# Column tiles for the small matmuls of a segment loop, a whole output projection, and a shorter last segment

## The chip, the cores and the metric

The kernel runs on one core of a Trainium2 chip. The metric is the device time in microseconds of one execution.

## The reference

Two branches read the same `x` (2048 tokens of 512): a recurrent attention `A` and a feed-forward `B`, mixed by a gate. Only `A` bears on this case. It goes through 64 segments of 32 tokens, and each segment needs the 8 memory rows that the previous one produced.

```python
mem = mem0                                    # 8 rows
for s in range(64):
    h = concat([mem, x[32*s : 32*s+32]])      # 40 rows
    q, k, v = h @ Wq, h @ Wk, h @ Wv          # 32 heads of 128
    p = softmax(mask(q @ k.T * scale))
    o = (p @ v) @ Wo                          # 4096 -> 512
    mem = o[:8]                               # needed by the next segment
    outs.append(o[8:])
return g * concat(outs) + (1 - g) * B(x)      # B: layernorm, two linear layers, gelu
```

## The kernel before

Each pass of the loop handles one segment. What is needed for the next memory comes first, and other work (output projections of the tokens, projections of later tokens, the branch `B`) fills the gaps as "side work". TensorE writes its results into banks of a memory called PSUM, and VectorE, ScalarE or GpSimd copy or work on them; one engine tells another that it is done through a semaphore, a counter that the other waits for. Four segments make one tile of 128 tokens, and `si` is the segment's place in its tile. The parts that the change and the argument touch, in the order in which TensorE runs them:

```python
# first sums: softmax denominators of the memory rows (one 128x128 tile)
nc.tensor.matmul(sm[:], lhsT=BO[:], rhs=E[:, :, 8:16], start=True, stop=False)
nc.tensor.matmul(sm[:], lhsT=BO[:], rhs=E[:, :, 0:8], start=False, stop=True)
run_fill(5 + (si == 3))                                   # side work
nc.vector.reciprocal(out=R[:, 0:8 * NG]..., in_=sm[:])
nc.vector.tensor_tensor(out=Pm[...], in0=E[..., 0:16], in1=R[...], op=ALU.mult)
av(Um, 8, s, V, Pm, 8, 0, 0)                              # value product, 32x128 tiles
# second sums: denominators of the other rows, into the mask's bank (bank 7)
nc.tensor.matmul(sr, lhsT=BO[:], rhs=E[:, :, 16:48], ...)
nc.tensor.matmul(sr[:, :, 24:32], lhsT=BO[:], rhs=E[:, :, 48:56], ...)
...                                                       # UTT <- Um, four copies
nc.vector.reciprocal(out=R[:, 8 * NG:]..., in_=sr)        # 256 columns
for half in range(2):                                     # projection of the memory rows, two halves
    wp = bank((nb, nd)[half], [P, 256])
    for u in range(8):
        wo_unit(wp, UTT[Tp % 2], ..., 256 * half, 256 * half + 256)   # 128x32 tiles
    (nc.scalar.copy if half else nc.vector.tensor_copy)(out=wsb[:, d], in_=wp[:])
S_next = mask_mm()                                        # mask into bank 7, one 128x128 tile
av_x(s - 1, ...)                                          # value product of the other rows
run_fill(2 * (si == 3))
for m in range(KC):                                       # memory output, four 128x128 tiles
    nc.tensor.matmul(aT[:, m, :], lhsT=wsb[:, m * P:(m + 1) * P], rhs=Sel[:, 0:M], ...)
nc.vector.tensor_copy(out=hn[:, :, 0:M], in_=aT)          # hT: the next segment's memory
for _ in fill: pass                                       # rest of the side work
```

## Time and profile before

| | before |
|---|---|
| median time | 835.74 us (3 runs, 835.13 to 835.79) |
| span of the profiled execution | 832.9 us |
| TensorE busy | 804.7 us, 97% |
| mean iteration, mask to mask | 11.19 us |
| from the last segment's first projection to the end | 26.6 us |

The mean iteration leaves out the first four. The last row of the table is 832.9 minus 806.32, the start of the last segment's first projection. A 97% busy TensorE says only that a matmul is always in flight. What is lost shows in the distances between starts where the tile shape changes. The prediction below shows those lines.

### The profile page before, as it was taken

What the parts mean: (1) busy time and instruction counts of PE and PEld (TensorE: products, weight loads), DVE (VectorE), ACT (ScalarE), POOL (GpSimd) and SP (SyncE); (2) the same over time, 40 slices, a digit from 0 to 9 for tenths busy, and PEclk for the clock granted to TensorE, in tenths of its full rate; (3) what the DMA queues carried; (4) which work ended last, traced back from release to release, by engine and by line L of the source; (5) the groups of instructions that cost most, each with busy time, mean ns of one, the idle gap of its engine ahead of it and who ended that gap; (6) DMA issues with size and microseconds to landing.
All of it is one profiled execution on the core that took longest, in us unless ns stands there. A gap on an engine that the chain in (4) does not pass through costs nothing.

```text
span 832.9 us, 49239 instructions
## 1 busy us (share of the span) xinstructions
PE 804.7 (97%) x22405; PEld 495.4 (59%) x22417; DVE 501.7 (60%) x1019; ACT 434.0 (52%) x1245; POOL 273.7 (33%) x625
## 2 busy tenths in 40 slices
PE   6999999999999999999999999999999999999886
PEld 4665555665666665566566556656656656665554
DVE  5764256565666566666656565656656665666553
ACT  3555544555455555555554555455555555555552
POOL 8000234242424333332424242434243243424220
PEclk9999999999999999999999999999999999999999
DMA  9791210100000010101010100000010101010000
GB/s 318 253 391 44 87 32 7 28 12 24 15 23 23 17 28 10 37 11 35 10 27 13 35 11 22 23 20 26 12 34 10 36 10 35 5 35 5 10 5 24
DMA packets 38216, 37.64 MB, mean 45 GB/s; under 512 B 13545, under 2 KB 36434, under 8 KB 36466
## 3 DMA queue, kind: packets, MB, share of 16 engines
q1 hardware_dynamic: 37874, 34.31, 12.4%
q8 instruction: 177, 2.90, 1.5%
q14 instruction: 37, 0.30, 0.1%
q0 software_dynamic: 128, 0.13, 0.1%
HBM read 26.03 MB, written 6.29 MB: 39 GB/s over the span
## 4 chain that ended last, share of the span: by engine, by line
PE 93%; DVE 3%; DMA 1%; issue 1%; SPq 1%; ACT 1%; DVEq 0%; ACTq 0%
PE b L211 35%; PE b L233 18%; PE b L222 17%; PE b L384 5%; PE hp L456 4%; PE bp L473 4%; PE b L360 2%; PE b L369 2%; PE b L684 2%; PE b L719 1%; PE b L389 1%; PE b L673 1%; DMA Wo_sb<-in_A_x_dram 1%; PE b L320 1%; PE b L373 0%
## 5 line engine op out<-in xcount | busy, mean ns | idle before, releaser
L217 DVE STREAM_TRANSPOSE Tt<-b 128x512 f32<-128x512 f32 (+1 forms) x384 | 225.6, 613 | 85.5 <-PE b L211 71.8
L211 PEld LDWEIGHTS <-hT 128*32 128x32 bf16 x5120 | 134.7, 97 | 100.0 <-DVE hT L720 15.4
L233 PE MATMUL b<-Wo_sb,UTT 128*32 128x256 bf16 (+1 forms) x4736 | 162.7, 285 | 1.2 <-ACT UTT L619 0.8
L222 PE MATMUL b<-Wv_sb,hT 128*32 128x512 bf16 x2048 | 141.9, 379 | 0.0
L211 PE MATMUL b<-Wq_sb,hT 128*32 128x512 bf16 x2048 | 132.9, 380 | 1.4 <-DVE hT L720 1.4
L211 PE MATMUL b<-Wk_sb,hT 128*32 128x256 bf16 (+1 forms) x3072 | 133.3, 308 | 0.0
L233 PEld LDWEIGHTS <-UTT 128*32 128x32 bf16 x4736 | 121.4, 97 | 19.1 <-ACT UTT L619 1.5
L654 ACT CAST KT<-Tt 128x256 bf16<-128x256 f32 (+1 forms) x192 | 87.1, 476 | 53.6 <-DVE Tt L217 53.6
L605 POOL TENSOR_TENSOR Px<-E,R 128x256 bf16<-128x256 bf16 x64 | 43.0, 672 | 218.7 <-DVE R L689 218.7
L689 DVE RECIPROCAL R<-b 128x256 f32<-128x256 f32 x64 | 112.5, 1757 | 0.0
L654 POOL CAST QT<-Tt 128x512 bf16<-128x512 f32 x64 | 39.1, 611 | 192.6 <-DVE Tt L217 192.6
L619 ACT CAST UTT<-b 128x256 bf16<-128x256 f32 x256 | 76.8, 387 | 23.9 <-PE b L389 23.4
L708 ACT CAST wsb<-b 128x256 bf16<-128x256 f32 x66 | 24.6, 372 | 120.1 <-PE b L233 120.1
L677 DVE RECIPROCAL R<-b 128x64 f32<-128x64 f32 x64 | 35.6, 557 | 79.4 <-PE b L674 79.4
L654 ACT CAST QT<-Tt 128x512 bf16<-128x512 f32 x64 | 39.6, 619 | 66.7 <-DVE Tt L217 66.7
L384 PEld LDWEIGHTS <-V 32*128 32x128 bf16 x4096 | 35.3, 91 | 46.2 <-DVE Pm L679 32.0
L222 PEld LDWEIGHTS <-hT 128*32 128x32 bf16 x2048 | 49.5, 96 | 21.1
L688 ACT CAST UTT<-b 128x64 bf16<-128x64 f32 x128 | 20.9, 215 | 75.2 <-PE b L389 75.2
L461 ACT ACTIVATE hg<-hp,b_sb 128x256 bf16<-128x256 f32 x80 | 37.7, 473 | 38.9 <-PE hp L456 38.9
L456 PE MATMUL hp<-yT,w_sb 128*128 128x256 bf16 (+1 forms) x352 | 53.8, 278 | 2.8 <-ACT hg L461 1.5
L607 POOL TENSOR_TENSOR racc<-racc,R 128x320 f32<-128x320 f32 x64 | 55.5, 867 | 0.0
L720 DVE CAST hT<-b 128x32 bf16<-128x32 f32 x63 | 12.1, 191 | 62.4 <-PE b L719 61.6
(116 smaller groups left out, 1075.2 us busy)
## 6 DMA issues: line engine op xcount, KB each, us to landing
Wv_sb<-in_A_Wv_dram SPq DMA_DIRECT2D x4, 1024.0 KB
Wq_sb<-in_A_Wq_dram SPq DMA_DIRECT2D x4, 1024.0 KB
Wk_sb<-in_A_Wk_dram SPq DMA_DIRECT2D x4, 1024.0 KB
Wo_sb<-in_A_Wo_dram SPq DMA_DIRECT2D x2, 2048.0 KB
vd<-vt SPq DMA_DIRECT2D x32, 128.0 KB
vs<-vd SPq DMA_DIRECT2D x256, 16.0 KB
out_dram<-o SPq DMA_DIRECT2D x16, 128.0 KB
Wo_sb<-in_A_x_dram SPq DMA_DIRECT2D x1, 1024.0 KB
```

The costliest lines, as they stand in the source:

```text
L211: nc.tensor.matmul(bk[32 * j:32 * j + 32, 0:n], lhsT=G[:, kc, :], rhs=W5[t][:, kc, h0:h1, j, :], start=(kc == 0), stop=(kc == KC - 1), til ...
L217: nc.vector.transpose(out=Tt[:, 0:n], in_=bk[:, 0:n])
L222: nc.tensor.matmul(bk[32 * j:32 * j + 32, :], lhsT=G[:, kc, :], rhs=Wv5[:, kc, 4 * vb:4 * vb + 4, j, :], start=(kc == 0), stop=(kc == KC - ...
L233: nc.tensor.matmul(bk[32 * g:32 * g + 32, :], lhsT=ut[:, i, j, c0:c0 + 32], rhs=Wo_sb[:, 4 * i + j, d0:d1], start=(j == 0 and i < 4), stop ...
L384: nc.tensor.matmul(U[j][:, i, :], lhsT=V[q, i, :], rhs=Pt[q, i, c_main:c_main + n], start=(i == 0), stop=False, skip_group_check=True, til ...
L456: nc.tensor.matmul(hp[:rows, :], lhsT=w1_sb[:, kc, fc * P:fc * P + rows], rhs=yTs[blk][:, kc, :], start=(kc == 0), stop=(kc == KC - 1))
L461: nc.scalar.activation(out=hg_[:rows, :], in_=hp[:rows, :], func=ACTF.Gelu_apprx_tanh, bias=b1_sb[:rows, fc:fc + 1], scale=1.0)
L605: nc.gpsimd.tensor_tensor(out=Px[:, :, 0:32], in0=E[:, :, 16:48], in1=Rr, op=ALU.mult)
L607: nc.gpsimd.tensor_tensor(out=racc[:], in0=racc[:], in1=R[:], op=ALU.add)
L619: nc.scalar.copy(out=UTT[T % 2][:, :, j, c0 + M:c0 + 40], in_=U[:])
L654: (nc.gpsimd.tensor_copy if bi == 2 else nc.scalar.copy)(out=dst, in_=Tv)
L689: nc.vector.reciprocal(out=R[:, 8 * NG:].rearrange("p (i q) -> p i q", q=32), in_=sr)
```

## The change

TensorE loses 0.10 to 0.11 us where the tile shape changes (the prediction reads this off the lines), and the loop mixed three shapes: 128x32 for the projections, 32x128 for the value products, 128x128 for sums, mask and memory output. The change writes those last three as 128x32 tiles. It also makes the memory projection one pass of 512 columns instead of two of 256, cuts the product `Pm` in two so that its first half is ready sooner, and reworks the end: the last segment computes no memory (nobody reads it), its output projections run in line, and the last output leaves in two column halves.

```diff
+    def sums(o, rhs, start, stop):
+        for j in range(4):
+            q = slice(32 * j, 32 * j + 32)
+            nc.tensor.matmul(o[q], lhsT=BO[:, q], rhs=rhs, start=start, stop=stop, ..., tile_position=(0, 32 * j))
+    def mem_out(aT, wsb):
+        for m in range(KC):
+            for c in range(4):
+                nc.tensor.matmul(aT[32 * c:32 * c + 32, m, :], lhsT=wsb[:, m * P + 32 * c:m * P + 32 * c + 32], rhs=Sel[:, 0:M], ..., tile_position=(0, 32 * c))
     def mask_mm():
-        nc.tensor.matmul(S, lhsT=ident[:], rhs=MkA[:]..., start=True, stop=True)
+        for j in range(4):                                    # q as in sums
+            nc.tensor.matmul(S[q], lhsT=ident[:, q], rhs=MkA[:]..., tile_position=(0, 32 * j))
 ... in the loop
-            nc.tensor.matmul(sm[:], lhsT=BO[:], rhs=E[:, :, 8:16], start=True, stop=False)   # and three more
+        sums(sm, E[:, :, 8:16], True, False)                                                 # and three more
-            nc.vector.tensor_tensor(out=Pm[...], in0=E[:, :, 0:16]..., in1=R..., op=ALU.mult)
+        for c in (8, 0):
+            nc.vector.tensor_tensor(out=Pm[:, :, c:c + 8], in0=E[:, :, c:c + 8], in1=R[:, 0:8 * NG]..., op=ALU.mult)
-        for half in range(2): ... wo_unit(wp, ..., 256 * half, 256 * half + 256)
-            (nc.scalar.copy if half else nc.vector.tensor_copy)(out=wsb[:, d], in_=wp[:])
+        wp = bank(nb, [P, Dm])
+        for u in range(8):
+            wo_unit(wp, UTT[Tp % 2], 24 - 8 * sp, u)
+        nc.scalar.copy(out=wsb[:], in_=wp[:])
-            for m in range(KC): nc.tensor.matmul(aT[:, m, :], lhsT=wsb[:, m * P:(m + 1) * P], ...)
+            mem_out(aT, wsb)
 ... the PSUM banks are taken in another order, as the projection now needs one in place of two
 ... the last segment leaves the loop after its scores; some 60 lines of its own end follow
```

## The prediction

> **What bounds the kernel now.** I read the page first (busy shares, then the chain that ended last), then the timeline of TensorE, VectorE and ScalarE over one inner iteration, then the groups by shape for the durations.
>
> ```profile
> PE 804.7 (97%) x22405; PEld 495.4 (59%) x22417; DVE 501.7 (60%) x1019; ACT 434.0 (52%) x1245; POOL 273.7 (33%) x625
> PE 93%; DVE 3%; DMA 1%; issue 1%; SPq 1%; ACT 1%; DVEq 0%; ACTq 0%
> ```
>
> TensorE is busy for 97% of the span and is 93% of the chain. No other engine is near. So the question is how much of TensorE's time is streaming and how much is something a different tiling can remove. One iteration (one segment of 32 tokens, about 11.2 us; 64 of them) in TensorE's timeline; columns are start us, length us, instruction, count:
>
> ```profile
> 520.26 0.82 PE L222 MATMUL b<-Wv_sb,hT 128*32 128x512 bf16 x12
> 521.01 0.20 PE L673 MATMUL b<-E,BO 128*128 128x64 bf16 x1
> 521.05 0.19 PE L674 MATMUL b<-E,BO 128*128 128x64 bf16 x1
> 521.18 1.05 PE L211 MATMUL b<-Wq_sb,GL 128*32 128x512 bf16 x16
> 522.05 0.39 PE L211 MATMUL b<-Wk_sb,GL 128*32 128x512 bf16 x4
> 522.37 0.36 PE L384 MATMUL b<-Pm,V 32*128 32x8 bf16 x32
> 522.59 0.23 PE L389 MATMUL b<-Pm,VL 32*128 32x32 bf16 x8
> 522.75 0.28 PE L684 MATMUL b<-E,BO 128*128 128x256 bf16 x1
> 522.87 0.19 PE L685 MATMUL b<-E,BO 128*128 128x64 bf16 x1
> 522.99 0.40 PE L211 MATMUL b<-Wk_sb,GL 128*32 128x512 bf16 x4
> 523.22 1.92 PE L233 MATMUL b<-Wo_sb,UTT 128*32 128x256 bf16 x64
> 525.07 0.36 PE L360 MATMUL b<-MkA,ident 128*128 128x448 bf16 x1
> 525.37 0.37 PE L384 MATMUL b<-Px,V 32*128 32x32 bf16 x32
> 525.58 0.24 PE L389 MATMUL b<-Px,VL 32*128 32x32 bf16 x8
> 525.75 0.26 PE L719 MATMUL b<-Sel,wsb 128*128 128x8 bf16 x4
> 525.94 0.62 PE L211 MATMUL b<-Wk_sb,GL 128*32 128x512 bf16 x8
> ```
>
> To be seen: four column-tiled (128*32) matmuls run side by side, since 16 of 512 columns (521.18 to 522.05) take 0.87 us, 0.216 per wave of four. A wave of 256 columns takes 0.109: 16 waves of L233 are 1.75 us. Now compare starts where the tile shape changes. L222's three waves should end at 520.26 + 0.65 = 520.91, but L673 (128*128) starts at 521.01: 0.10 late. L233 should hand over at 524.97; the mask L360 starts at 525.07: 0.10 late. L360's 448 columns stream in 0.19, but L384 (32*128) follows after 0.30: 0.11 late. L685's 64 columns (0.03) take 0.12. Where the shape stays (L211 to L233) nothing is lost. So each change of tile shape costs about 0.1 us, and there are nine per iteration.
>
> **What the Trainium skill says.** "TensorEngine Tiling (Array Packing)", Tiling Modes, Key Properties: "Changing tiling mode (not just tile) drains the TensorE". The trace agrees and gives the size: 0.10 to 0.11 us. "TensorE: Matmul & The Clock Gate", Part 3, says tiles in different column groups run concurrently; it agrees (0.216 us for four of 512). "ScalarE: Activation LUTs", What ACT_TABLE_LOAD costs, gives 0.833 ns per element; the page's groups agree, 372 ns for a 256-column copy out of PSUM and 585 for 512, the difference being 256 x 0.83. "VectorE: DVE Perf Modes", TRN2 errata, gives (N+151)/0.96 ns for a two-input fp32 operation: 291 at N=128, trace 292; so I take 225 ns for N=64.
>
> The waits that can replace a removed switch are in these lines of VectorE and then ScalarE over the same stretch:
>
> ```profile
> 521.28 0.56 DVE L677 RECIPROCAL R<-b 128x64 f32<-128x64 f32 x1 [1.64 <-PE b L674]
> 521.95 0.29 DVE L679 TENSOR_TENSOR Pm<-E,R 128x128 bf16<-128x128 bf16 x1
> 522.88 0.36 DVE L688 CAST UTT<-b 128x64 bf16<-128x64 f32 x2 [0.65 <-PE b L389]
> 523.17 1.76 DVE L689 RECIPROCAL R<-b 128x256 f32<-128x256 f32 x1
> ```
>
> ```profile
> 520.73 0.19 ACT L670 ACTIVATION_READ_ACCUMULATOR E<-b 128x1 f32 x1
> 525.19 0.37 ACT L708 CAST wsb<-b 128x256 bf16<-128x256 f32 x1 [1.95 <-PE b L233]
> ```
>
> **The change part by part, per iteration.** The sums (L673, L674, L684, L685), the mask (L360) and the memory output (L719) become 128*32 tiles, four matmuls in place of one, same columns, so the streaming time is the same. Of nine switches five go: into and out of the first sums, out of the second sums, into the mask, out of the memory output. Four stay, around the two value products (L384/L389). Five times 0.1 is 0.5 us; times 63 iterations, 31 us. That is the ceiling. What is left of each, in the order of the timeline:
>
> (a) First sums. Entry: 0.106 goes, but E's accumulator read ends at 520.92 and a consumer follows a release by about 0.055 (the hT copy ends 526.24, its weight load starts 526.29), so the sums can start at 520.975 in place of 521.01: 0.035. Exit: 0.16 from L673 to the next L211 becomes 0.04 + 0.02: 0.10. Together 0.135. The next value product needs Pm. VectorE's reciprocal starts with the sums, 0.035 earlier, and the product is cut in two, only the first half (225 ns) needed at once: Pm at 522.14 + 0.055, TensorE free at 522.24. So 0.135 is kept, except in every fourth iteration, where GpSimd copies VL at the same time and the product takes 0.40 (its product of 128 columns is 403 ns there): about 0.05.
>
> (b) Second sums. 0.104 goes between L684 and L233. But L233 needs the UTT copy: VectorE's first one ends near 523.11 and L233's load starts 0.055 later, 523.16, for a matmul at 523.22. Only 0.055 is kept.
>
> (c) Whole projection. 8 waves of 512 in place of 16 of 256: same streaming. The start of the last wave comes 0.13 earlier (7 x 0.216 + 0.01 = 1.52 against 1.65). Before, half 0 left during half 1 and only 372 ns of ScalarE lay behind the end. Now all 512 columns do: from the last start 0.45 to ScalarE's start (a 512-column matmul record is 0.38, and L708 starts 0.07 after such an end), 0.585 copy, 0.06 to the weight load. So memory output at 1.52 + 0.45 + 0.585 + 0.06 = 2.62 after the first L233, against 525.75 - 523.22 = 2.53. The mask's saved switch vanishes into this wait and 0.09 is lost. In the iteration with si = 3 two units of fill (0.44 us) stand between and cover the copy; there the mask waits for VectorE's 1.76 us reciprocal, which frees its bank: it starts at 2.35 after the value product in place of 2.435, and with the fill's switch (0.106) gone too, (b) and (c) together give 0.20.
>
> (d) Memory output. 16 small matmuls at 6 ns take 0.09 as the four did; the 0.08 of the switch out of it is saved. The hT chain behind it (matmul 0.17, copy 0.19, waits) is 0.45, the two units of fill 0.46: it just fits. With si = 3 one unit of fill is left and hT binds as before: 0.
>
> Sum for four iterations (si = 0, 1, 2, 3): 0.18 + 0.18 + 0.10 + 0.33 = 0.79 us. 63 iterations: 12.4 us.
>
> (e) The end. Before, from the last segment's first projection (806.3) to TensorE's last load of the check flag (827.3) are 21.0 us, with several stretches of TensorE waiting on ScalarE and VectorE. Adding the new order up with the same durations (no memory part; three projections of 1.73, the last output in two halves of 0.87; ScalarE copies of 0.585 between them; the check's count done early) I get 19.2. So 1.7 us; the 5.6 us behind it stay.
>
> (f) Scattered stalls of 0.2 to 0.4 us on TensorE ("issue" before L384, some 3 us in all) stay; where they fall before the memory output the new wait hides them: perhaps 0.5 us.
>
> Total 12.4 + 1.7 + 0.5 = 14.6 us: 835.7 - 14.6 = 821.1.
>
> **Rivals.** First: the waits behind the switches are softer than I read them, and most of the 0.5 us is kept. For it: every saved switch also shifts the work that feeds the waits. Against it: E, UTT and wsb hang on ScalarE and VectorE, whose lines show 0.035, 0.055 and less than nothing of slack. It would give 805 to 812. Second: the exposed copy costs more than 0.09 (ScalarE at 0.63 as in its back-to-back copies, or hT missing its fill by a hair), in three of four iterations, and eats the rest: 826 to 833. For it: (d) fits by 0.01 us only. Third: VectorE becomes the bound through the mask's bank, in all iterations. Against it: the wait for wsb comes 0.1 later than that one. It would change nothing in the sum. Fourth: only the end gets faster (834).
>
> **Range and chances.** The sum is made of terms of 0.05 to 0.1 us repeated 63 times, so an error of 0.05 us per iteration is 3 us. I take 821 with 816 to 826. Faster by over 2% means under 819.0, which needs 2 us more than I find: 0.28. Within 2%: 0.70. Slower: 0.02.
>
> **What would show it.** In the after trace: L673's successors start 0.03 us earlier against ScalarE's read, followed by fill with no gap; the weight loads of the memory output wait for ScalarE's wsb copy in three iterations of four, 0.1 to 0.2 us each, with that copy at 0.585 us; L233's load waits for UTT; the mask waits for the reciprocal in si = 3; a mean iteration (mask to mask) of about 11.02 us in place of 11.22. I am wrong if the memory output does not wait for wsb (then 812 or less), or if the new tiles themselves take longer than the ones they replace.

## The result and the profile after

| | before | after |
|---|---|---|
| median time (same rounds, 4 runs each) | 835.51 us | 822.74 us (822.18 to 822.87) |
| span of the profiled execution | 832.9 us | 821.1 us |
| mean iteration, mask to mask | 11.19 us | 11.03 us |
| last segment's first projection starts at | 806.32 us | 796.54 us |
| from there to the end | 26.6 us | 24.6 us |

The output is correct. The ratio is 0.9846 (95% interval 0.9829 to 0.9863): 1.5% faster, within the 2% that was called "same". Ratios here are the mean time of one kernel's fast runs over that of the other's in the same rounds, so not quite the ratio of the medians. In the traces the span fell by 11.8 us, 9.8 of them in the loop and 2.0 in the end. The medians fell by 12.8; each kernel has one trace, and the last microsecond is not assigned. (In the loop itself, from the first segment's first projection to the last one's, it is 10.1 us; the stretch before the loop took 0.3 us longer.)

First the busy line and the chain's first line of the page of the kernel after:

```profile
PE 793.0 (97%) x22013; PEld 443.4 (54%) x22013; DVE 493.1 (60%) x1022; ACT 446.6 (54%) x1239; POOL 272.7 (33%) x624
PE 92%; DVE 4%; issue 1%; DMA 1%; SPq 1%; ACT 1%; DVEq 0%; ACTq 0%
```

TensorE is as busy as before, and the number of matmuls is even a little lower: the halved projection saved more than the tiles added. The share of VectorE in the chain rose from 3% to 4%: this fits waits that take the place of switches. Now TensorE's timeline over the segment that the prediction shows (columns: start, length, instruction, count):

```profile
515.11 0.82 PE L222 MATMUL b<-Wv_sb,hT 128*32 128x512 bf16 x12
515.83 0.24 PE L360 MATMUL b<-E,BO 128*32 128x64 bf16 x8
515.88 1.05 PE L211 MATMUL b<-Wq_sb,GL 128*32 128x512 bf16 x16
516.75 0.40 PE L211 MATMUL b<-Wk_sb,GL 128*32 128x512 bf16 x4
517.08 0.36 PE L398 MATMUL b<-Pm,V 32*128 32x8 bf16 x32
517.30 0.23 PE L403 MATMUL b<-Pm,VL 32*128 32x32 bf16 x8
517.46 0.32 PE L360 MATMUL b<-E,BO 128*32 128x256 bf16 x8
517.60 0.39 PE L211 MATMUL b<-Wk_sb,GL 128*32 128x512 bf16 x4
517.87 1.91 PE L233 MATMUL b<-Wo_sb,UTT 128*32 128x512 bf16 x32
519.71 0.37 PE L374 MATMUL b<-MkA,ident 128*32 128x448 bf16 x4
520.02 0.37 PE L398 MATMUL b<-Px,V 32*128 32x32 bf16 x32
520.23 0.24 PE L403 MATMUL b<-Px,VL 32*128 32x32 bf16 x8
520.47 0.27 PE L365 MATMUL b<-Sel,wsb 128*32 128x8 bf16 x16
520.59 0.60 PE L211 MATMUL b<-Wk_sb,GL 128*32 128x512 bf16 x8
521.06 1.05 PE L211 MATMUL b<-Wq_sb,hT 128*32 128x512 bf16 x16
```

Read it against the prediction's block. The first sums (now L360) and the side work after them follow at once: from the start of the last V matmuls (L222) to the side work, 0.77 us instead of 0.92. After the second sums and the four side matmuls, the projection L233 comes 0.27 after 517.60, which is four matmuls of 512 columns (0.216) and a wait of 0.05. Before the memory output there is a hole: the last value product L403 starts at 520.23, and L365 only at 520.47, 0.24 later; before, it was 0.17 (525.58 to 525.75), and that contained the switch. What fills the hole is in the lines of ScalarE, the second view below; first those of VectorE:

```profile
516.12 0.56 DVE L692 RECIPROCAL R<-b 128x64 f32<-128x64 f32 x1 [1.62 <-PE b L360]
516.78 0.36 DVE L695 TENSOR_TENSOR Pm<-E,R 128x64 bf16<-128x64 bf16 x2
517.59 0.36 DVE L703 CAST UTT<-b 128x64 bf16<-128x64 f32 x2 [0.45 <-PE b L403]
517.90 1.76 DVE L704 RECIPROCAL R<-b 128x256 f32<-128x256 f32 x1
520.82 0.19 DVE L721 CAST hT<-b 128x32 bf16<-128x32 f32 x1 [1.15 <-PE b L365]
```

In the kernel before, the hT copy was this line:

```profile
526.05 0.19 DVE L720 CAST hT<-b 128x32 bf16<-128x32 f32 x1 [0.85 <-PE b L719]
```

Then ScalarE and the weight loads that follow (two views of the kernel after):

```profile
519.84 0.59 ACT L711 CAST wsb<-b 128x512 bf16<-128x512 f32 x1 [1.88 <-PE b L233]
```

```profile
520.47 0.17 PEld L365 LDWEIGHTS <-wsb 128*32 128x32 bf16 x16
521.06 0.12 PEld L211 LDWEIGHTS <-hT 128*32 128x32 bf16 x8 [0.37 <-DVE hT L721]
```

The copy of wsb ends at 519.84 + 0.59 = 520.43, and the weight load of the memory output starts 0.04 later. The reciprocal L704, which reads bank 7, ends at 517.90 + 1.76 = 519.66, and the mask, which writes bank 7, starts at 519.71. The hT copy ends at 521.01 and the next segment's weights are loaded at 521.06. So the wait for wsb stands where the prediction put it. The mask's wait is there in every iteration (52 to 53 ns from the reciprocal's end to the mask in all), not only with si = 3. The wait for hT, which the prediction had as just covered by side work except with si = 3, now sets the next projection with every si: it starts 0.05 us after the copy's end, where before that was 0.14 with si = 0 to 2 and 0.05 with si = 3 only. The view of waits (total us, times, longest) of the kernel before and then of the kernel after shows the last of them grow:

```profile
DVE hT L720 <- PE b L719: 61.6, 62, 1.7
PEld L211 <- DVE hT L720: 15.4, 61, 0.4
```

```profile
DVE hT L721 <- PE b L365: 79.0, 63, 1.7
PEld L211 <- DVE hT L721: 23.5, 61, 0.5
PEld L233 <- DVE UTT L703: 12.2, 63, 0.3
```

The weight loads of the next projection wait 23.5 us for hT, 8 us more than before. The prediction's sum has no such wait with si = 0 to 2, though its second rival names it.

Last the end. TensorE before, then after:

```profile
818.31 1.93 PE L233 MATMUL b<-Wo_sb,UTT 128*32 128x256 bf16 x64
821.00 2.11 PE L233 MATMUL b<-Wo_sb,UTT 128*32 128x256 bf16 x64 [0.75 <-ACT UTT L619]
826.00 0.40 PE L324 MATMUL b<-wsbL,SelL 128*32 128x512 bf16 x4 [0.53 <-ACT wsbL L311]
826.22 0.16 PE L744 MATMUL b<-good 128*1 128x1 bf16 x1
```

```profile
806.54 0.17 PE L802 MATMUL b<-good 128*1 128x1 bf16 x1
807.90 0.40 PE L320 MATMUL b<-wsb,SelX 128*32 128x512 bf16 x4 [1.19 <-DVE bad L804]
811.66 3.66 PE L233 MATMUL b<-Wo_sb,UTT 128*32 128x512 bf16 x96 [0.91 <-ACT UTT L763]
815.91 0.29 PE L786 MATMUL b<-wsbL,SelL 128*32 128x256 bf16 x4 [0.27 <-DVE wsbL L775]
```

The new end has two waits of its own, of 1.19 us behind the early check and 0.91 us for UTT. The last matmul comes 19.4 us after the last segment's first projection (815.91 - 796.54) instead of 19.9 (826.22 - 806.32), and what follows it is shorter too.

### What one iteration gave, step by step

"Stall-free" lengths are medians over the undisturbed iterations of each kind (10 to 13 in these two kernels), from one next-segment projection to the next:

| us per iteration | si = 0 | 1 | 2 | 3 | sum |
|---|---|---|---|---|---|
| predicted gain | 0.18 | 0.18 | 0.10 | 0.33 | 0.79 |
| measured gain | 0.18 | 0.16 | 0.08 | 0.23 | 0.65 |

63 iterations are 15.75 such fours, so 0.65 makes 10.2 us where 12.4 were predicted. (The first iterations and the last three are of other lengths, so this does not add up with the stalls to the 10.1 us exactly.)

### Stalls of TensorE

Apart from the modal iteration, TensorE sometimes stops for 0.1 to 0.9 us where nothing in the trace makes it wait. I count as a stall each place where two successive matmul starts are over 0.1 us further apart than the median of the same place in iterations of the same kind. The first four iterations and those of unusual length in instructions are left out. Before has 10 stalls (3.1 us in all), after 8 (2.6 us). They turn out to matter in the experiments.

### The profile page after: what moved, and what is told of

Read it like the earlier page. It is cut to its first block, busy times and chain, and to the rows that moved or that the text cites. A ratio compares the mean times of both kernels' runs of the same rounds, so it can differ in the third digit from the quotient of the medians.

```text
span 821.1 us, 48437 instructions
## 1 busy us (share of the span) xinstructions
PE 793.0 (97%) x22013; PEld 443.4 (54%) x22013; DVE 493.1 (60%) x1022; ACT 446.6 (54%) x1239; POOL 272.7 (33%) x624
## 4 chain that ended last, share of the span: by engine, by line
PE 92%; DVE 4%; issue 1%; DMA 1%; SPq 1%; ACT 1%; DVEq 0%; ACTq 0%
PE b L211 33%; PE b L233 18%; PE b L222 16%; PE b L398 5%; PE hp L470 4%; PE bp L487 4%; PE b L360 3%; PE b L374 2%; PE b L365 2%; PE b L383 2%; PE b L403 1%; DVE R L692 1%; DMA Wo_sb<-in_A_x_dram 1%; DVE Pm L695 1%; PE b L387 0%
## 5 line engine op out<-in xcount | busy, mean ns | idle before, releaser
L211 PEld LDWEIGHTS <-hT 128*32 128x32 bf16 x5120 | 131.3, 97 | 108.2 <-DVE hT L721 23.5
L233 PE MATMUL b<-Wo_sb,UTT 128*32 128x512 bf16 (+1 forms) x2656 | 160.9, 378 | 1.3 <-ACT UTT L763 0.9
L222 PE MATMUL b<-Wv_sb,hT 128*32 128x512 bf16 x2048 | 141.8, 378 | 0.0
L704 DVE RECIPROCAL R<-b 128x256 f32<-128x256 f32 x63 | 110.7, 1757 | 0.0
L233 PEld LDWEIGHTS <-UTT 128*32 128x32 bf16 x2656 | 64.4, 96 | 63.8 <-DVE UTT L703 12.2
L711 ACT CAST wsb<-b 128x512 bf16<-128x512 f32 x63 | 36.9, 586 | 111.2 <-PE b L233 111.2
L634 ACT CAST UTT<-b 128x256 bf16<-128x256 f32 x248 | 74.4, 386 | 9.7 <-PE b L403 7.5
L222 PEld LDWEIGHTS <-hT 128*32 128x32 bf16 x2048 | 49.4, 96 | 21.2
L721 DVE CAST hT<-b 128x32 bf16<-128x32 f32 x63 | 12.1, 191 | 79.0 <-PE b L365 79.0
```

The source lines that it names most:

```text
L211: nc.tensor.matmul(bk[32 * j:32 * j + 32, 0:n], lhsT=G[:, kc, :], rhs=W5[t][:, kc, h0:h1, j, :], start=(kc == 0), stop=(kc == KC - 1), til ...
L222: nc.tensor.matmul(bk[32 * j:32 * j + 32, :], lhsT=G[:, kc, :], rhs=Wv5[:, kc, 4 * vb:4 * vb + 4, j, :], start=(kc == 0), stop=(kc == KC - ...
L233: nc.tensor.matmul(bk[32 * g:32 * g + 32, :], lhsT=ut[:, i, j, c0:c0 + 32], rhs=Wo_sb[:, 4 * i + j, d0:d1], start=(j == 0 and i < 4), stop ...
L634: nc.scalar.copy(out=UTT[T % 2][:, :, j, c0 + M:c0 + 40], in_=U[:])
L704: nc.vector.reciprocal(out=R[:, 8 * NG:].rearrange("p (i q) -> p i q", q=32), in_=sr)
```

## The experiments

All twelve give correct results. They ran in three batches of four, each batch with its own runs of the kernel before (medians 835.46, 835.10, 834.72 us), on three chips. Each is the kernel after with one edit, unless it says otherwise.

| run | median us | ratio to before | span us | dense stretch | stalls, us in all | of them behind a packet |
|---|---|---|---|---|---|---|
| before | 834.72 to 835.51 | 1 | 832.9 | 218 | 10, 3.1 | 7 |
| after | 822.74 | 0.9846 | 821.1 | 184 | 8, 2.6 | 4 |
| e1_halves | 830.73 | 0.9949 | 829.7 | 248 | 28, 12.1 | 26 |
| e2_old_mask | 822.58 | 0.9845 | 820.8 | 178 | 9, 2.1 | 1 |
| e3_old_mem | 823.63 | 0.9862 | 821.8 | 160 | 4, 1.3 | 0 |
| e4_old_sums | 830.32 | 0.9944 | 828.4 | 184 | 4, 1.3 | 0 |
| e5_tail_only | 834.13 | 0.9987 | 831.9 | 218 | 12, 4.0 | 8 |
| e6_split_copy | 830.31 | 0.9941 | 828.9 | 184 | 5, 1.3 | 3 |
| e7_one_pm | 824.85 | 0.9880 | 822.6 | 184 | 5, 1.2 | 2 |
| e8_extra_rows | 844.30 | 1.0112 | 842.2 | 216 | 4, 1.3 | 0 |
| e9_vl_later | 821.43 | 0.9842 | 819.0 | 184 | 6, 1.8 | 3 |
| e10_sums_only_halves | 824.70 | 0.9884 | 822.4 | 218 | 11, 4.3 | 10 |
| e11_rows_before_wo | 826.67 | 0.9906 | 825.1 | 216 | 12, 4.3 | 8 |
| e12_vl_later_old_mask | 820.79 | 0.9833 | 819.1 | 178 | 5, 1.6 | 1 |

"Dense stretch" is the number of TensorE's instructions, a weight load and a matmul for each, from the first matmul of the memory projection (in e11 of the 16 extra ones before it) to the last of the memory output. For the kernel after that is 2 x (32 + 4 + 40 + 16) = 184. The last column counts the stalls that end 1.2 to 1.65 us after the end of a 16 KiB packet of the instruction queue; both are explained with e1, e10 and e11.

Half the width of the intervals of the ratios is 0.0013 to 0.0017, 1.1 to 1.4 us. The kernel after was not rerun inside the batches, so where two of these kernels are compared within 2 us, the iteration lengths in the traces decide and not the medians.

### Which tiles carry the gain: e4, e3, e2

e4_old_sums puts the four sums back as 128x128 matmuls:

```diff
-        for j in range(4): nc.tensor.matmul(o[q], lhsT=BO[:, q], rhs=rhs, ..., tile_position=(0, 32 * j))
+        nc.tensor.matmul(o, lhsT=BO[:], rhs=rhs, ...)
```

> The changed kernel with both sums as 128*128 matmuls again. Theory: nearly the whole gain of the loop comes from them. First sums 0.143 us in three iterations of four and 0.04 in the fourth, second sums 0.055 us in three of four (in the one with si = 3 the wait for the reciprocal hides it): 0.63 us per four iterations, 10 us in all: 832.7. Rival: all five removed switches share the gain evenly, then two of the ten sides are theirs and the run is 5 to 6 us slower: 828.

Measured: 830.32 us. The stall-free iterations are longer by 0.57 us per four (9.0 us in all), and it has 1.3 us less of stalls. The difference, 7.7, is what the time shows (830.32 - 822.74 = 7.6). Most of the loop's gain comes from the sums; the miss against 832.7 is partly the stalls, which the expectation left alone.

e3_old_mem puts the four-matmul memory output back:

```diff
-            for c in range(4): nc.tensor.matmul(aT[32 * c:32 * c + 32, m, :], lhsT=wsb[:, m * P + 32 * c:...], ..., tile_position=(0, 32 * c))
+            nc.tensor.matmul(aT[:, m, :], lhsT=wsb[:, m * P:(m + 1) * P], rhs=Sel[:, 0:M], ...)
```

> The changed kernel with the memory output as four 128*128 matmuls again. The prediction's step (d) says 0.08 us in three iterations of four would be lost: 3.8 us slower, 826.5. The trace of the changed kernel says otherwise: from the first memory matmul to the next projection it takes 0.60 us in place of 0.63 in three iterations and 0.604 in place of 0.540 in the fourth, since VectorE sees the end of the 16 small matmuls 38 to 65 ns later; so about 0.02 us per four iterations: 822.7 to 823.5. If the old form is really the faster one in the fourth iteration, the trace shows 0.54 there again.

Measured: 823.63 us, 0.9 more than the kernel after and within the intervals; in no case the 3.8 of the prediction's step (d). Iterations are 0.14 us longer per four (2.2 us), stalls 1.3 us shorter. The expectation had 0.02 per four: it left out that with si = 3 the switch into the memory output comes back too (0.66 us from the last value product to it instead of 0.55). Its own test came true: from the first memory matmul to the next projection the trace shows 0.63 us with si = 0 to 2 and 0.54 with si = 3, as in the kernel before. The waits of the kernel with the old memory output tell why:

```profile
DVE hT L719 <- PE b L364: 76.3, 63, 1.6
PEld L211 <- DVE hT L719: 15.5, 62, 0.4
```

With four 128x128 matmuls the wait for hT is 15.5 us, as it was in the kernel before (15.4); with sixteen small column tiles it is 23.5. Half of the switch saved behind the memory output (with si = 3 more than all of it) is paid back in the wait for its result.

e2_old_mask puts the one-matmul mask back:

```diff
-        for j in range(4): nc.tensor.matmul(S[q], lhsT=ident[:, q], rhs=MkA[:]..., tile_position=(0, 32 * j))
+        nc.tensor.matmul(S, lhsT=ident[:], rhs=MkA[:]..., start=True, stop=True)
```

> The changed kernel with the mask as one 128*128 matmul again. Theory: the mask waits for VectorE's long reciprocal in every iteration (0.31 us from the last L233 to the mask where 0.205 is natural), so the removed switch of 0.105 us was only turned into that wait; putting it back costs nothing: 822.7 within 0.5 us. Rival: every switch on TensorE costs its 0.105 us: 63 x 0.105 = 6.6 us slower, 829.3.

Measured: 822.58 us: the tiled mask is worth nothing. It waits for the reciprocal in bank 7 in every iteration, and the switch fits inside that wait.

### The halved product and the collision with GpSimd: e7, e9, e12

e7_one_pm puts `Pm` back as one product of 128 columns:

```diff
-        for c in (8, 0): nc.vector.tensor_tensor(out=Pm[:, :, c:c + 8], ...)
+        nc.vector.tensor_tensor(out=Pm[...], in0=E[:, :, 0:16]..., in1=R...unsqueeze(2).to_broadcast([P, NG, 2, 8]), op=ALU.mult)
```

> The changed kernel with Pm in one product again. In the trace Pm's first half is ready 0.015 us before TensorE needs it (0.072 us from its end to the value product, 0.057 at the least), and the whole product takes 0.067 longer: 0.05 us lost for si = 0 and 1, and as much for si = 2 (0.403 in place of 0.357); nothing for si = 3. So 0.15 us per four iterations, 2.4 us: 825.1. Rival: the split was worth nothing, 822.7.

Measured: 824.85 us, as expected. Without the split the value product starts 0.05 to 0.06 us later after the side work with si = 0 to 2; the iterations are 0.17 us longer per four (2.7 us, expected 2.4), and stalls are 1.4 us shorter.

In one iteration of four the first half of Pm is slow. The kernel after, GpSimd and then VectorE, at such a place:

```profile
526.86 1.04 POOL L299 COPY VL<-vs 128x1024 bf16<-128x1024 bf16 x1
```

```profile
527.62 0.59 DVE L695 TENSOR_TENSOR Pm<-E,R 128x64 bf16<-128x64 bf16 x2
```

The two halves take 0.59 us instead of 0.36. In 13 of the 14 such places where the two meet, the first half ends 72 to 76 ns after GpSimd's copy does (in the other it starts only when the copy is done). It is not merely slowed: it is held until the copy ends. e9_vl_later issues that copy, and the loads beside it, later:

```diff
-        if si == 3 and T + 1 < NT: left_v_in(T + 1)        # at the start of the iteration
-        if si == 3 and T + 2 < NT: x_left(T + 2)
 ...                                                        # after the QT and KT copies:
+        if si == 3 and T + 1 < NT: left_v_in(T + 1)
+        if si == 3 and T + 2 < NT: x_left(T + 2)
```

> The changed kernel with GpSimd's copy of VL (and the loads beside it) issued later in every fourth iteration, behind its copy into QT. Theory: in those iterations (16 of 64) the first Pm half takes 357 ns in place of 226 because GpSimd works on SBUF at the same time, and the start of the fill to the value product is 0.425 us in place of 0.311; moved away, 0.115 x 16 = 1.8 us come back: 820.9 us. Rival: the copy only collides with another VectorE product later in the iteration, or VL comes too late for the product that reads it: 822.7 or more.

Measured: 821.43 us. The same place in the trace of this run:

```profile
526.38 0.36 DVE L695 TENSOR_TENSOR Pm<-E,R 128x64 bf16<-128x64 bf16 x2
```

The iterations concerned (si = 2; the program issues the copy with si = 3, but GpSimd is ahead there) fell from 10.95 to 10.83 us, and the medians of the others stayed. 14 such places make 1.7 us; stalls are 0.9 us shorter, which is not the copy's doing as far as is known, and the span fell by 2.1. The median is 1.3 us below the kernel after's, but the ratio moved only from 0.9846 to 0.9842. The mechanism is shown in the trace; the gain in time is not resolved.

e12_vl_later_old_mask adds the one-matmul mask to e9 (both diffs are above).

> The later VL copy together with the mask as one matmul: 192 fewer matmuls. The tiled mask was worth nothing by itself (822.58 without it), so theory: the sum of the two, 820.7, possibly 0.3 less if fewer instructions mean fewer stalls. Rival: as the changed kernel, 822.7.

Measured: 820.79 us, ratio 0.9833, the fastest of all. It beats the kernel before by 1.7%. Against the kernel after its iterations are shorter (the one kind by 0.12 us), but their intervals overlap.

### The end alone: e5

e5_tail_only is the kernel before, whole loop included, with the new end:

```diff
-    for s in range(nseg + 2):
+    for s in range(nseg):            # the last segment leaves after its scores
+    ... the new end, with its sums in 128x32 tiles
```

> The kernel before with only the changed end: no memory part in the last segment, its projections in line, the last output in two column halves; the 63 iterations of the loop as before. Theory: from the last segment's first projection to the end the traces take 24.6 us after and 26.6 before, so 2.0 us less than before: about 833.5. Rival: the end hides behind the branch and the output's landing that follow, then 835 as before.

Measured: 834.13 us, ratio 0.9987, interval 0.9974 to 1.0001. In its trace the end takes 24.5 us (807.42 to 831.9) instead of 26.6, so 2.1 us shorter. Its stalls are 0.9 us longer than before's, so about 1 us is left to see, and that agrees.

### The whole projection: e1, e6

e1_halves projects in two halves again, with the copies and the order of PSUM banks of the kernel before (the lines for the order are left out):

```diff
-        wp = bank(nb, [P, Dm])
-        for u in range(8): wo_unit(wp, UTT[Tp % 2], 24 - 8 * sp, u)
-        nc.scalar.copy(out=wsb[:], in_=wp[:])
+        for half in range(2):
+            wp = bank((nb, nd)[half], [P, 256])
+            for u in range(8): wo_unit(wp, ..., 256 * half, 256 * half + 256)
+            (nc.scalar.copy if half else nc.vector.tensor_copy)(out=wsb[:, d], in_=wp[:])
```

> The changed kernel with the projection of the memory rows again in two halves of 256 columns (VectorE copies the first, ScalarE the second, banks as before). Theory from the traces: the whole projection is a loss inside this change, since its 586 ns copy is exposed and TensorE's memory output waits 0.07 us for it in three iterations of four. With halves the memory output starts when the value product ends, 2.53 us after the first L233 in place of 2.60, so 47 x 0.07 = 3.3 us less, minus 0.2 us in the others: about 819.6 us. Rival: halving the weight loads and matmuls was itself worth something (64 pairs to 32 per iteration), then this run is 1 to 3 us slower than 822.7.

Measured: 830.73 us, and neither theory fits. The stall-free iterations, here from mask to mask and the shortest first, are the same as the kernel after's (10.77, 10.94, 11.04, 11.22 us; after 10.78, 10.96, 11.04, 11.22). The memory output does start 0.07 us earlier after the mask (0.69 instead of 0.76), but the distance from its last matmul to the next segment's first grows from 0.49 to 0.55. So undoing the exposed copy wins nothing back. The wait for hT takes its place: VectorE's hT copy starts 0.30 us after the last memory matmul instead of 0.24, the next projection starts 0.05 us after that copy in both kernels, and the view of waits of this run shows as much waiting for hT as the kernel after's (23.5):

```profile
PEld L211 <- DVE hT L723: 24.6, 59, 0.5
```

What costs 8 us is something else: 28 stalls with 12.1 us, 9.4 more than after. One of them in TensorE's timeline of this run:

```profile
233.66 0.37 PE L374 MATMUL b<-MkA,ident 128*32 128x448 bf16 x4
233.97 0.32 PE L398 MATMUL b<-Px,V 32*128 32x32 bf16 x24
234.50 0.22 PE L398 MATMUL b<-Px,V 32*128 32x32 bf16 x8 [0.21 <-issue]
```

In the middle of a value product, between its 24th and 25th matmul, TensorE stops, and the profile has no releaser for it ("issue").

e6_split_copy keeps the whole projection and splits only the copy between ScalarE and VectorE:

```diff
-        nc.scalar.copy(out=wsb[:], in_=wp[:])
+        nc.scalar.copy(out=wsb[:, 0:256], in_=wp[:, 0:256])
+        nc.vector.tensor_copy(out=wsb[:, 256:Dm], in_=wp[:, 256:Dm])
```

> The changed kernel, whole projection kept, but its copy out of PSUM split: columns 0 to 255 by ScalarE, 256 to 511 by VectorE, at the same time. Same instructions on TensorE. If the memory output's wait for wsb is what costs (the prediction's step c), it starts 0.07 us earlier in 47 iterations: 3.3 us less, 819.4. If VectorE's view of the memory output (the hT copy, released later when the 16 small matmuls come straight behind the value product, as the first run with halves showed) takes the place of that wait, it is 0 to 1 us less: 822.

Measured: 830.31 us, and it failed as a test. Its trace, all engines, around the memory output:

```profile
445.62 0.37 ACT L711 CAST wsb<-b 128x256 bf16<-128x256 f32 x1 [1.88 <-PE b L233]
446.02 0.42 DVE L712 CAST wsb<-b 128x256 bf16<-128x256 f32 x1 [0.57 <-ACT wsb L711]
446.50 0.12 PEld L365 LDWEIGHTS <-wsb 128*32 128x32 bf16 x8 [0.18 <-DVE wsb L712]
```

VectorE's copy waits for ScalarE's instead of running beside it. The two read one PSUM tile and write one SBUF tile (SBUF is the memory for operands). It is hardly the second that orders them: in the kernel after, ScalarE's half of the UTT copies runs beside VectorE's (517.59, above), into one SBUF tile and from separate PSUM tiles:

```profile
517.63 0.33 ACT L703 CAST UTT<-b 128x64 bf16<-128x64 f32 x2 [0.96 <-PE b L403]
```

In e6, 0.37 and 0.42 one after the other are more than the 0.59 of one copy, and the second half of the memory output waits in the middle. To split such a copy, separate PSUM tiles would be the thing to try; no run here did that with a whole projection.

### What the stalls are: e8, e10, e11

The traces suggest an answer. The instruction queue q8 moves packets of 16384 bytes, and 26 of the 28 stalls of e1 end 1.2 to 1.65 us after the end of such a packet. The page's line on that queue (packets, MB, share), of the kernel before, of the kernel after, and of e1:

```profile
q8 instruction: 177, 2.90, 1.5%
```

```profile
q8 instruction: 174, 2.85, 1.5%
```

```profile
q8 instruction: 189, 3.10, 1.5%
```

The Trainium skill, page "Runtime: NRT & Kernel Launch", section Instruction fetch mechanics, says that each engine's instructions come in 16 KiB blocks of 256, fetched while the current block runs, and that crossing a block is mostly hidden. The counts agree: 24,029 matmuls and as many weight loads make 48,058 instructions, 188 blocks, against 189 packets. In e1 it may not be hidden: in its dense stretch it issues 248 of TensorE's instructions in 2.6 us, nearly a whole block; the kernel after issues 184 in 2.7. The packets before those 26 stalls take 0.9 to 1.5 us (median 1.1), and TensorE resumes 1.4 us after their end (median), together 2.5 us, about as long as the dense stretch. So my theory was that TensorE outruns its instruction supply where many small matmuls stand close together. The rival: stalls depend on where block limits happen to fall.

e8_extra_rows adds 16 small matmuls ahead of the mask, into unused columns of its bank:

```diff
+        for z in range(4):
+            for j in range(4):
+                nc.tensor.matmul(B[q, NG * EW:NG * EW + M], lhsT=BO[:, q], rhs=Sel[:, 0:M], ..., tile_position=(0, 32 * j))
         S_next = mask_mm()
```

> The changed kernel with 16 more weight loads and 16 more 8-column matmuls per iteration, into unused columns, placed where TensorE waits 0.105 us for the reciprocal anyhow. Theory from the first run with halves (28 stalls of 12 us in TensorE, each ending about 1.4 us behind the end of a 16 KB packet of the instruction queue, against 8 stalls of 2.6 us in the changed kernel, with equal undisturbed iterations): TensorE's instruction fetch does not keep up when the short matmuls are too many, so this run gets more such stalls: 3 to 6 us slower, 826 to 829, at iterations that are otherwise as long as those of the changed kernel. Rival: the stalls came from the halves themselves (VectorE's copy, the banks); then 822.7 to 823.5.

Measured: 844.30 us, with 4 stalls and 1.3 us. The test was badly built:

```profile
520.63 0.27 PE L717 MATMUL b<-Sel,BO 128*32 128x8 bf16 x16
520.99 0.37 PE L374 MATMUL b<-MkA,ident 128*32 128x448 bf16 x4
```

The extra matmuls write bank 7, so they too wait for the reciprocal, and the mask now comes 0.36 us behind them. Every iteration is 0.36 us longer. That slack is also time for a fetch, so the few stalls speak for neither side.

e11_rows_before_wo puts the same 16 where nothing new is waited for, ahead of the projection and in its own bank:

```diff
         wp = bank(nb, [P, Dm])
+        for z in range(4):
+            for j in range(4):
+                nc.tensor.matmul(wp[q, 0:M], lhsT=BO[:, q], rhs=Sel[:, 0:M], start=(z == 0), ..., tile_position=(0, 32 * j))
```

> The changed kernel with 16 more weight loads and 8-column matmuls per iteration, put just ahead of the whole projection and in its own bank, which the projection then overwrites; they wait for nothing new, and TensorE waits there for the UTT copies anyway. 23,021 matmuls, as many as in the run of extra rows that slowed every iteration by 0.36 us and had 4 stalls. By the length of iterations without stalls: 0 to 0.1 us more each, 0 to 6 us. Theory that stalls come with instructions per microsecond: in addition 14 to 20 stalls and 4 to 6 us more than the changed kernel's 2.6 us, so 827 to 834. Rival: stalls stay at 4 to 10, 1.5 to 3 us, and the time is what the modal iterations say, 823 to 829.

Measured: 826.67 us. Stall-free iterations are 0.12 us longer per four (1.9 us), and there are 12 stalls with 4.3 us, 1.7 us more than after. Together 3.6, against 3.9 in the medians. The stalls rose, 8 of them behind a packet instead of 4, but by less than the theory's 4 to 6 us.

e10_sums_only_halves takes the sums alone from the change, with mask, memory output and halves as before (the diffs of e1, e2 and e3 together):

> The changed kernel with only the sums tiled: mask, memory output and the projection in halves as in the kernel before. It has 23,084 matmuls in about 825 us, between the kernel before (22,405, 10 stalls of TensorE, 3.1 us in all) and the run with halves and all tiles (24,029, 28 stalls, 12.05 us). Lengths of iterations without stalls: 0.14 per four above the changed kernel's (old memory output), so 822.7 + 2.2 = 824.9 with few stalls. Theory that the stalls grow with instructions per microsecond: about 16 stalls, 7 us, so 829. Rival, that they belong to where instructions happen to lie in the program and not to their number: any count, and then about 825 if it is as before.

Measured: 824.70 us. A first count gave 29 stalls; 18 of them sat in one iteration whose matmul starts are shifted by one place against the others, as when a record is missing, and that iteration is left out. What stays is 11 stalls with 4.3 us, 10 of them behind a packet. The stall-free iterations came out as long as after's (43.98 us per four against 44.00), not 0.14 longer. With 1.7 us more of stalls that makes 1.4; the span rose by 1.4 and the median by 2.0. The theory's direction held, its 16 stalls and 7 us were too many, and its time of 829 was wrong.

What follows from the table: the one run with 248 instructions in the dense stretch has 26 stalls behind a packet. The four with 216 or 218 that do not wait in the stretch (before, e5, e10, e11) have 7 to 10. All with 184 or fewer have 0 to 4. e8 has 216 but waits 0.36 us longer inside, and has none; e11 with the same number of matmuls in the same loop has 8. So the stalls go with how densely instructions stand in that stretch, and not with their number in the program. That the supply of instructions is the cause is argued from the packets and not shown, since no run changed the fetch alone. e1, with most stalls, and e10 also put the old bank order back; the kernel before has that order and 10 stalls, so it is not enough by itself. The other stalls, 1 to 8 in a run, have no explanation here.

## Why the prediction was right, and where it was not

The time predicted was 821.0 us, with 816 to 826, and 822.74 came out. Of 14.6 us predicted, 12.8 came (11.8 in the traces). The mechanism was right in (a), (b), (c) and (e), wrong in (d), and (f) came out by luck. The loop was put 2 us too high, and the microsecond of the medians that no trace assigns brings the total nearer than the steps are. By its steps, with medians from TensorE's starts:

- **(a) First sums: right.** The distance from the last V matmul to the side work fell from 0.473 to 0.330 us, 0.143 (predicted 0.135), and was kept except with si = 2, where 0.06 was left (predicted 0.05), because of the VL copy as named. Pm's first half takes 226 ns elsewhere, for the 225 taken. e4 shows that the sums carry most of the loop, e7 that the cut in Pm is needed for it.
- **(b) Second sums: right.** 0.582 to 0.526 from the last value matmul to the projection: 0.056 (predicted 0.055). The wait for UTT bounds it, 12.2 us in 63 waits.
- **(c) Whole projection: right in the iteration.** First projection matmul to memory output went from 2.535 to 2.601 us, a loss of 0.066 (predicted 0.09). In si = 3, (b) and (c) together gave 0.163 where 0.20 was predicted: the mask came at 2.37 us after the value product and not at 2.35, the side work behind it gave 0.097 and not 0.106, and the prediction's own terms (0.085 + 0.106) add up to 0.19. But e1 shows that undoing it would not give the loss back, and that its worth is one that the prediction did not name: together with all the tiles, halves make TensorE stall 9.4 us more, and with the sums' tiles alone (e10) 1.7 us more.
- **(d) Memory output: this step failed.** "The 0.08 of the switch out of it is saved" and, for si = 3, "hT binds as before: 0". In fact 0.04 was saved in si = 0 to 2 (0.628 to 0.587 us from the memory output to the next projection), and in si = 3 0.064 was lost (0.540 to 0.604). The step took the time from matmul to copy as unchanged. It was not: from the start of the last memory matmul to VectorE's hT copy there were 206 ns before and 244 after (271 in si = 3), with a matmul record of 166 ns in both.

  So a sign of being wrong that the prediction named came true in part: the new tiles take longer than the old. The semaphore that tells VectorE is updated 14 to 17 ns after the end of the record of the last 128x128 matmul, 28 to 29 after four column tiles, and 54 to 81 after the sixteen small ones. The Trainium skill has this, "TensorE: Matmul & The Clock Gate", The cost: per-tile semaphore tail: 25 + 4.7 for each tile + 26.3 for each increment, in ns. From 1 to 4 tiles that is an estimate of +14 (the trace: +15), from 1 to 16 of +70 (the trace: +40 to +67). I had read the neighbouring section for the streaming and not this one.

  But the number of tiles is not all: behind the same sixteen matmuls the update comes 110 ns after the record in e1 (+96), where they follow the value product at once, and 54 in the kernel after, where a wait for wsb lies between. The ends of matmul records are modelled, so the traces don't tell whether the signal is late or the matmuls themselves; why it differs stays open. e3 shows that the sixteen tiles are what delays the copy: with four matmuls it starts 204 ns after the last again, and the wait for hT is back at 15.5 us. This step accounts for nearly all of the shortfall in si = 3 together with the 0.04 in (b) and (c).
- **(e) The end: right,** 2.0 us in the trace and 2.1 in e5, predicted 1.7 (its own 21.0 - 19.2 is 1.8). TensorE's part went to 19.4 us, and the 5.6 us behind it, which were to stay, became about 5.1.
- **(f) Stalls: the size came by luck,** 0.5 us less (3.1 to 2.6). That waits hide them is not shown: other runs with the same waits for wsb have 1.2 to 4.3 us of stalls; the experiments tie many of them to how densely instructions are issued.

Of the rivals, the third came true as it was put: VectorE's reciprocal holds the mask in all iterations and changes nothing (e2). The second had its mechanism, hT missing its fill by a hair, but its size was 0.04 to 0.06 us and not enough for 826. The first and the fourth fell. Of the signs named beforehand, the exposed copy (586 ns in the page's group) and the waits for wsb and UTT came, that for wsb shorter than the 0.1 to 0.2 us named: with si = 0 to 2 the weight load always follows the copy's end by 0.05 us, but had stood idle for only 0.09 to 0.10. The mean iteration of 11.02 us (11.03 measured) came by luck, since it was counted down from 11.22 where the trace has 11.19: 0.16 was gained, not 0.20. The mask's wait came in all iterations and not only in si = 3.

## What to carry to other kernels

Count the tile switches for the ceiling, then read at each switch which semaphore would bind next: here five switches of 0.1 us were worth 0.5 us, and 0.16 was kept. A matmul cut into many small ones can stream as fast and still be seen later by the engine that waits for it (0.04 to 0.09 us here), so measure before tiling the one whose result is on the chain. And count instructions too: in a dense stretch of small matmuls, fewer and longer ones can save more than any switch (8 us between e1 and the kernel after).

## What the Trainium skill lacked or had wrong

- "TensorEngine Tiling (Array Packing)", Key Properties, says that a change of tiling mode drains TensorE and gives no size. In this kernel it is 0.10 to 0.11 us per change.
- "Runtime: NRT & Kernel Launch", Instruction fetch mechanics, calls the fetch of instructions hidden or mostly hidden. With 248 instructions of TensorE in 2.6 us, 28 stalls with 12.1 us came up, 26 of them ending 1.2 to 1.65 us after a 16 KiB packet of the instruction queue; with 184 in 2.7 us it was 8 with 2.6 us, 4 of them behind a packet. The link to the fetch is likely and not proven, and no page tells how to see it in a profile.
- "TensorE: Matmul & The Clock Gate", per-tile semaphore tail, was close in size for four column tiles (+15 ns against +14). For sixteen 8-column matmuls in four column groups, +40 to +67 ns were seen where its formula gives +70 for sixteen tiles, and +96 in e1, where they follow a change of tile shape at once. It does not say whether matmuls that reuse a column group count as new tiles, nor that what stands before them matters.
